# A fused attention and expert kernel: the last two units' means, values and products in another order, and a place of its own for unit 15's x

## The chip, the cores and the metric

The kernel runs on one core of a Trainium2 chip. The time is device time in microseconds (us) of one execution; the median of three is given. Engines are named as the profile names them: PE (TensorE, matmuls and transposes), DVE (VectorE), ACT (ScalarE), POOL (GpSimd) and SP (SyncE, which here only issues DMAs). SPq, ACTq and POOLq are the DMA issues of these engines.

## What is computed

Two stages, in float32:

```python
# attention: batch 8, heads 8, sequence 576, head size 64
q_d, k_d, v_d = means of q, k, v over 4 neighbours       # 144 rows
out = repeat(softmax(q_d k_d / 8) v_d, 4) + softmax(q k / 8, |i - j| < 4 only) v
x   = out.transpose(0, 2, 1, 3).reshape(4608, 512)
# experts: 4 groups of 4; every token goes to one
g   = argmax(x @ w_group);  e = argmax(x @ w_expert[g])
y   = softmax weights of both choices * (relu(x @ w1[g, e]) @ w2[g, e])
```

The result is y, 4608 x 512.

## The kernel before

**Attention by units.** The work of attention is cut into 16 units (2 batches and 2 heads each), numbered 0 to 15. A unit goes through named steps: scores (`s_local`, `s_down`), exponentials, and then, as far as it matters here:

- `down_store u` (L443) writes the unit's mean output `odn` to a table `odd` in DRAM: three DMAs on SP, two of 64 KB and one of 16 KB. `load_down u` (L450) reads it back in another layout, one DMA of 144 KB into eight-row strips of the tile `vw`.
- `load_windows u` (L211) loads the unit's values into the other rows of the same tile: two DMAs on SP of 378 KB each. Units 14 and 15 use the tiles vw0 and vw1.
- `turn_e u i` (L375) transposes a third of the local softmax weights `E` on PE, and `turn_e_out` copies it to `pt`. `x_bank u i` (L455) multiplies that third with `vw`: these are the value products, and since the means stand in `vw` as further rows, they add both parts of attention. `x_bank_out u i` (L464) copies the product to the tile `x`, `store_x` (L467) writes `x` to the DRAM table `xd`, and `turn_x`, `turn_x_out`, `logits` (L472 to L508) make the router's scores of it.

So `x_bank u` needs both `load_windows u` and `load_down u`, and `load_down u` can only be issued when `down_store u` has landed.

**The first expert, early.** When 12 units are in `xd`, 256 tokens of one small expert are fetched (`gather`, two indirect DMAs on POOL, L919) while attention still runs. `weights_in c` (L881) loads a quarter of the expert's two weights: two DMAs of 512 KB on SP, into two buffers that take turns. `weights_split c w` (L888) makes a high part on ACT (L891) and a low part on POOL or DVE (L892). `turn_in k` (L962) transposes a quarter of the tokens on PE, and ACT and DVE split it into `xh` and `xl` (L959, L960). `hidden f` (L971) is twelve matmuls on these; its third one, and every third, reads the low part of the weight. `project f` follows. Then the other 15 experts run in a loop that keeps PE busy to the end.

**What sets the order.** The string `ORDER` (L1387) names every step of attention, router and first expert in the order in which its instructions are recorded; each engine and each DMA queue then does its own instructions strictly in that order, with semaphores between the engines. A letter behind a step names the engine that copies (A, D, P) or the queue that issues (S is SP, A is ACT). Where a step waits, everything that is recorded behind it on the same engine waits too.

**Places.** `of(n, u)` (L114) picks the buffer of a unit: for units 14 and 15 it is always the first, so `x` of unit 15 goes where `x` of unit 14 stands, and may be written only when `store_x 14` has read it. `change` in `ORDER` gives the space of attention's inputs to the expert's weights.

Of the kernel before, what the change touches and what calls it, by code (L numbers as in the profile page):

```python
# [9 lines left out]
F32 = mybir.dt.float32  # L10
# [9 lines left out]
P = 128  # L20
B, H, S, D = 8, 8, 576, 64
SD = S // 4
G = 9
W = 38
WW = 42
# [11 lines left out]
NU = 4 * NB  # L37
# [23 lines left out]
class Attention:  # L61
# [9 lines left out]
    def __init__(self, tc, q, k, vm, vw, idf, xd, left, right, dram):  # L71
        nc = self.nc = tc.nc
        self.tc, self.q, self.k, self.vm_in, self.vw_in, self.idf = tc, q, k, vm, vw, idf
        cp = self.cp = left.enter_context(tc.tile_pool(name="attc", bufs=1))
        self.a1 = left.enter_context(tc.tile_pool(name="att1", bufs=1))
        self.a2 = left.enter_context(tc.tile_pool(name="att2", bufs=2))
        self.inp = right.enter_context(tc.tile_pool(name="inp", bufs=2, side="right"))
        self.odd = [dram.tile([2, 2 * SD, D], F32, name=f"odd{i}") for i in range(2)]
        self.st, self.banks, self.lg = {}, {}, {}
        self.turns = 0  # L80
        self.xd = xd
        self.kt = [self.inp.tile([P, 2, S], F32, name=f"kt{i}", bufs=1) for i in range(3)]
        self.kz = [self.inp.tile([P, 2, 2, S + 6], F32, name=f"kz{i}", bufs=1) for i in range(2)]
        self.load_k(0)
        self.load_q(0)
        self.mask = self.inp.tile([P, G, W], BF16, name="mask", bufs=1)
        self.vw = [(cp if i < 2 else self.inp).tile([P, 2, 2 * NBLK, D], F32, name=f"vw{i}", bufs=1) for i in range(3)]
        self.warm = self.inp.tile([P, 4 * P], BF16, name="warm", bufs=1)
        nc.vector.memset(self.warm, 0.0)
        one = cp.tile([1, 1], F32, name="one")  # L90
        nc.gpsimd.memset(one, 0.0)
        nc.scalar.activation(one, one, AF.Exp)
        self.zero = cp.tile([P, 1], F32, name="zero")
        nc.gpsimd.memset(self.zero, 0.0)
        self.idb = cp.tile([P, P], BF16, name="idb")
        self.vd = [self.inp.tile([P, 3, 2, D], F32, name=f"vd{i}", bufs=1) for i in range(2)]
        self.vs = [self.inp.tile([P, 3, 2, 4 * D], F32, name=f"vs{i}", bufs=1) for i in range(3)]
        self.mg = [cp.tile([P, 5], F32, name=f"mg{i}") for i in range(2)]
        self.sg = [cp.tile([P, 5, 2], F32, name=f"sg{i}") for i in range(2)]
        self.sd = [cp.tile([P, 5], F32, name=f"sd{i}") for i in range(2)]  # L100
        self.sl = [cp.tile([P, G, 2], F32, name=f"sl{i}") for i in range(2)]
        self.two = [cp.tile([P, G, 2, 2], F32, name=f"two{i}") for i in range(2)]
        self.rg = [cp.tile([P, 6], F32, name=f"rg{i}") for i in range(2)]
        self.kept = {}
        for n, more, shape in (
            ("pt", 1, [P, G * P]), ("x", 2, [P, G, P]), ("PdT", 1, [P, 3, 2 * SD]), ("od", 1, [P, 2 * SD]), ("odn", 1, [P, 3, 2, D])
        ):
            self.kept[n] = [cp.tile(shape, F32, name=f"{n}0")] + [self.inp.tile(shape, F32, name=f"{n}{i + 1}", bufs=1) for i in range(more)]
        self.E = [cp.tile([P, G, WW, 3], F32, name=f"E{i}") for i in range(2)]
        self.shares = self.inp.tile([P, 8], F32, name="shares", bufs=1)  # L110
        self.xT = cp.tile([P, 27 * P // 2], F32, name="xT")
        self.edge = self.inp.tile([P, 3, W], F32, name="edge", bufs=1)

    def of(self, n, u):  # L114

        t = self.kept[n]
        return t[u % len(t) if u < LATE_UNITS else 0]

# [1361 lines left out]
turn_pd_out 14 1 A; turn_x 12 2; store_x 12 A; turn_x_out 12 2 A; load_windows 14; soft_down 14; out_down 14; x_bank 13 1; s_down_max 15  # L1480
weight 2; s_down_exp 15 2; out_down_out 14 A; turn_down 14; x_bank 13 2; s_down_exp 15 0; s_down_exp 15 1; x_bank_out 13 1 A; pool_v 15
x_bank 13 0; turn_pd 15 0; x_bank_out 13 2 A; turn_down_out 14; soft_local 14; x_bank_out 13 0 A; turn_pd_out 15 0 A; places_out 2
store_x 13 A; turn_pd 15 1; down_store 14 S; turn_x 13 2; turn_pd 15 2; turn_pd_out 15 1 A; logits 12; turn_pd_out 15 2 D; load_windows 15
s_local_exp 15 1; turn_x_out 13 2 A; out_down 15; lists_places 2; turn_x 13 0; soft_down 15; turn_x 13 1; lists 2 P; out_down_out 15 A
turn_down 15; turn_x_out 13 1 A; turn_down_out 15; turn_x_out 13 0 A; load_down 14 S; down_store 15 S; early_expert; lists_add 2
turn_e 14 2; logits 13; turn_e 14 1; early_list 1; turn_e_out 14 2 A; change; gather; turn_e 14 0; lists_out 2; turn_e_out 14 1 A
turn_e_out 14 0 A; x_bank 14 2; x_bank 14 0; x_bank 14 1; x_bank_out 14 0 A; x_bank_out 14 1 A; turn_x 14 0; soft_local_sum 15
soft_local 15; x_bank_out 14 2 D; turn_e 15 0; store_x 14 A; turn_e_out 15 0 D; turn_x_out 14 0 D; turn_x 14 2; turn_x 14 1
turn_x_out 14 1 D; turn_x_out 14 2 A; weights_in 0; turn_e 15 1; turn_in 0; turn_e_out 15 1 D; weights_split 0 w1 P; load_down 15 S
logits 14; turn_in 1; weights_split 0 w2 P; weights_in 1; turn_e 15 2; turn_e_out 15 2 D; x_bank 15 0; turn_in 2; x_bank_out 15 0 A  # L1490
x_bank 15 1; x_bank_out 15 1 A; x_bank 15 2; x_bank_out 15 2 D; turn_in 3; weights_in 2; turn_x 15 1; turn_x 15 2; turn_x_out 15 2 D
store_x 15 S; turn_x 15 0; weights_split 1 w1 P; turn_x_out 15 1 D; turn_x_out 15 0 A; hidden 0; weights_split 1 w2 P; weights_in 3
logits 15; scores_out 3; hidden 1; scores_turn 3; project 0; scores_turn_out 3; choose 3; choose_exp 3; choose_first 3; weight 3; hidden 2
project 1; places 3; places_out 3; project 2; weights_split 2 w1 P; lists_places 3; lists 3 P; count 3; weights_split 2 w2 P; hidden 3
hidden 4; hidden 5; lists_add 3; early_list 0; gather_late; weights_split 3 w1 D; project 3; weights_split 3 w2 D; project 4; ranks
project 5; hidden 6; turn_late 0; turn_late 1; hidden 7; turn_late 2; turn_late 3; rank_lists; project 6; project 7
"""

@with_exitstack
# [111 lines left out]
```

## Time and profile before

| what | us |
|---|---|
| median of 3 runs | 681.47 |
| lowest and highest of them | 678.83, 684.85 |
| the profiled execution | 675.84 |
| its span, first to last instruction | 674.1 |

The profile is of one execution, with starts in us from the beginning of its span. The order of a row is start, duration, engine, line, operation, destination and source, shapes and count; rows of like instructions that follow each other are merged. A bracket at the end of a row says how long the engine was idle ahead of it and what ended that idle time. The steps of the change lie between about 201 and 224 us.

### The profile page before, as it was taken

The page shows a single profiled execution, that of the slowest core. Times are in us where ns is not written, and L with a number is a line of the kernel's source. Part 1 is how long each engine was busy: PE and PEld are TensorE (multiplying, and loading weights), DVE is VectorE, ACT ScalarE, POOL GpSimd, SP SyncE. Part 2 cuts the span into 40 slices and gives each one's busy share as a digit, 9 for nine tenths or more (in the row PEclk, how much of TensorE's full clock was granted, in tenths as well). Part 3 has the DMA queues.
Part 4 walks back from the last instruction along what each step waited for, and adds up shares of the span by engine and source line. Part 5 has one row for each costly group of instructions (what it writes and reads, how often), then busy time and mean ns, then how long its engine had stood idle before and what let it go on. Part 6 is the DMA issues. An engine that isn't in the chain of part 4 may idle for free. (4 is left out here: it accounts for less than half of the span.)

```text
span 674.1 us, 17810 instructions
## 1 busy us (share of the span) xinstructions
PE 641.1 (95%) x6750; PEld 576.3 (85%) x6751; DVE 478.3 (71%) x968; ACT 385.1 (57%) x831; POOL 362.9 (54%) x418
## 2 busy tenths in 40 slices
PE   7899998998986998999999999999999999999996
PEld 3676776776764886999999999999999999999985
DVE  5888788788896695556566676766777777787751
ACT  7887757666773535653545346464565556566531
POOL 8974754668621733404464746557456557555521
PEclk8999999998999998899999999999999999999999
DMA  8699899898878635768786969889889889999920
GB/s 321 199 288 298 250 306 292 234 256 263 231 198 274 180 98 194 238 216 194 228 254 191 256 213 260 224 270 268 255 264 276 255 278 300 252 295 289 280 71 29
DMA packets 125903, 160.75 MB, mean 238 GB/s; under 512 B 23133, under 2 KB 90601, under 8 KB 125792
## 3 DMA queue, kind: packets, MB, share of 16 engines
q1 hardware_dynamic: 100032, 130.01, 64.0%
q0 software_dynamic: 8240, 20.47, 10.3%
q10 hardware_dynamic: 17520, 8.85, 4.9%
q8 instruction: 62, 1.02, 0.7%
q14 instruction: 49, 0.40, 0.2%
HBM read 129.51 MB, written 30.98 MB: 238 GB/s over the span
## 5 line engine op out<-in xcount | busy, mean ns | idle before, releaser
L1057 POOL DMA_INDIRECT out_dram<-yt,qo x135 | 156.2, 1157 | 134.4 <-DVE qo L838 102.7
L985 ACT ACTIVATE hh<-ph 128x368 fp32r<-128x368 f32 (+14 forms) x128 | 53.0, 416 | 183.0 <-PE ph L981 179.2
L981 PE MATMUL ph<-xh,w1h 128*128 128x368 f32 (+14 forms) x512 | 152.6, 299 | 0.0
L981 PE MATMUL ph<-xl,w1h 128*128 128x368 f32 (+14 forms) x512 | 152.4, 298 | 0.0
L981 PE MATMUL ph<-xh,w1l 128*128 128x368 f32 (+14 forms) x512 | 152.3, 298 | 0.0
L1032 PE MATMUL y<-hh,w2h 128*128 128x368 f32 (+11 forms) x416 | 126.1, 303 | 0.0
L1032 PE MATMUL y<-hl,w2h 128*128 128x368 f32 (+11 forms) x416 | 125.7, 302 | 0.0
L1032 PE MATMUL y<-hh,w2l 128*128 128x368 f32 (+11 forms) x416 | 125.6, 302 | 0.0
L986 DVE SCALAR_TENSOR_TENSOR hl<-ph,hh 128x368 fp32r<-128x368 f32 (+14 forms) x128 | 58.7, 461 | 78.0 <-ACT hh L985 77.6
L981 PEld LDWEIGHTS ph<-xh,w1h 128*128 128x128 f32 x512 | 96.4, 189 | 1.0 <-issue 0.2
L981 PEld LDWEIGHTS ph<-xl,w1h 128*128 128x128 f32 x512 | 96.5, 188 | 0.8
L981 PEld LDWEIGHTS ph<-xh,w1l 128*128 128x128 f32 x512 | 96.5, 188 | 0.1
L892 DVE TENSOR_TENSOR w1l<-raww,w1h 128x1024 fp32r<-128x1024 f32 x61 | 74.6, 1224 | 25.2 <-ACT w1h L891 24.6
L892 DVE TENSOR_TENSOR w2l<-raww,w2h 128x1024 fp32r<-128x1024 f32 x61 | 74.7, 1224 | 23.9 <-ACT w2h L891 22.9
L919 POOL DMA_INDIRECT xg<-xd,gi x47 | 54.0, 1149 | 55.2 <-ACT xh L959 25.3
L1032 PEld LDWEIGHTS y<-hh,w2h 128*128 128x128 f32 x416 | 78.3, 188 | 0.0
L1032 PEld LDWEIGHTS y<-hh,w2l 128*128 128x128 f32 x416 | 78.3, 188 | 0.0
L1032 PEld LDWEIGHTS y<-hl,w2h 128*128 128x128 f32 x416 | 78.3, 188 | 0.0
L891 ACT ACTIVATE w1h<-raww 128x1024 fp32r<-128x1024 f32 x64 | 67.3, 1052 | 7.2 <-DMA raww<-in_moe_w_dram 3.4
L891 ACT ACTIVATE w2h<-raww 128x1024 fp32r<-128x1024 f32 x64 | 67.1, 1050 | 0.0
L960 DVE TENSOR_TENSOR xl<-xt,xh 128x256 fp32r<-128x256 f32 (+16 forms) x68 | 30.4, 449 | 15.5 <-ACT xh L959 15.4
L460 PE MATMUL b_x<-vw,pt 126*32 126x128 f32 x1152 | 37.8, 275 | 2.1 <-DMA vw<-odd 1.6
(243 smaller groups left out, 1189.1 us busy)
## 6 DMA issues: line engine op xcount, KB each, us to landing
raww<-in_w2q_dram SPq DMA_DIRECT2D x52, 512.0 KB
raww<-in_w1q_dram SPq DMA_DIRECT2D x52, 512.0 KB
raww<-in_moe_w_dram SPq DMA_DIRECT2D x24, 512.0 KB
vw<-in_vw_dram SPq DMA_DIRECT2D x32, 378.0 KB
kt<-in_k_dram SPq DMA_DIRECT2D x16, 576.0 KB
qT<-in_q_dram SPq DMA_DIRECT2D x16, 576.0 KB
xd<-x ACTq DMA_DIRECT2D x15, 576.0 KB
vs<-in_vm_dram SPq DMA_DIRECT2D x16, 512.0 KB
```

The lines of the kernel that those rows point to most:

```text
L460: self.nc.tensor.matmul(pt[32 * j : 32 * j + 32, t], self.of("pt", u)[:ROWS, 32 * lin : 32 * lin + 32], self.windows(u)[:ROWS, :, lin], st ...
L891: self.nc.scalar.activation(hi, raw, AF.Copy)
L892: eng.tensor_tensor(out=lo, in0=raw, in1=hi.bitcast(F32), op=ALU.subtract)
L919: self.nc.gpsimd.indirect_dma_start(out=xg[:w], out_offset=None, in_=self.xd[0:rows], in_offset=bass.IndirectOffsetOnAxis(ap=st["gi"][:w, ...
L960: self.nc.vector.tensor_tensor(out=lo, in0=x, in1=hi.bitcast(F32), op=ALU.subtract)
L981: nc.tensor.matmul(ph, a[:, k, cs], st[b][:, k, 0:C], start=(n == 0), stop=(n == 11))
L985: nc.scalar.activation(hh, ph, AF.Relu)
L986: nc.vector.scalar_tensor_tensor(out=hl, in0=ph, scalar=0.0, in1=hh.bitcast(F32), op0=ALU.max, op1=ALU.subtract)
L1032: nc.tensor.matmul(y, a[:, f % 2, cs], b, start=(f == 0 and n == 0), stop=(f == 7 and n == 2))
L1057: i = self.nc.gpsimd.indirect_dma_start(out=out, out_offset=bass.IndirectOffsetOnAxis(ap=index, axis=0), in_=y, in_offset=None, bounds_che ...
```

## The change

Three things change, in the order string and in one buffer.

1. `load_windows 15` moves behind `load_down 14`, and `load_down 15` moves ahead of `weights_in 0` and `weights_in 1` (it stood between them). These are issues on SP's queue.
2. `x` of unit 15 goes into the space of `E0`, which unit 14 used and which is free once unit 14's `E` is transposed. `E0` grows from 1134 to 1152 floats per partition for that.
3. The value products, their copies and the transposes of units 14 and 15 stand in another order; all of `x_bank 15` stands ahead of `turn_in 0`, and `store_x 15` ahead of `weights_in 2`.

```diff
-        self.E = [cp.tile([P, G, WW, 3], F32, name=f"E{i}") for i in range(2)]
+        flat = [cp.tile([P, G * (P if i == 0 else 3 * WW)], F32, name=f"E{i}") for i in range(2)]
+        self.E = [x[:, 0 : G * 3 * WW].rearrange("p (g w e) -> p g w e", g=G, e=3) for x in flat]
+        self.last_x = flat[0].rearrange("p (g f) -> p g f", g=G)
...
     def of(self, n, u):
 
+        if n == "x" and u == NU - 1:
+            return self.last_x
...
-turn_x_out 14 1 D; turn_x_out 14 2 A; weights_in 0; turn_e 15 1; turn_in 0; turn_e_out 15 1 D; weights_split 0 w1 P; load_down 15 S
...
+turn_e 15 1; turn_e_out 15 1 A; turn_e 15 2; turn_e_out 15 2 A; turn_x_out 14 0 D; load_down 15 S; weights_in 0; weights_in 1; x_bank 15 0
+x_bank_out 15 0 A; x_bank 15 1; x_bank_out 15 1 D; logits 14; x_bank 15 2; x_bank_out 15 2 A; store_x 15 S; turn_in 0; weights_split 0 w1 P
...
```

The lines of the changed kernel are numbered four higher than those of the kernel before, from L120 on.

**SP's queue, before**, from the windows of unit 15 (vw1) to the first quarter of the weights (raww10 and raww20); odd0 and odd1 are the DRAM tables of the means of units 14 and 15:

```order
L214 DMA vw1_104<-in_vw_dram 42x2x1152 x2
L453 DMA vw0_103<-odd0_92 8x4x1152
L447 DMA odd1_93<-odn0_140 128x2x64 x2
L448 DMA odd1_93<-odn0_140 32x2x64
L1535 TENSOR_LOAD eri0_183
L1535 ISA x2
L886 ISA
L886 DMA raww10_3839<-in_moe_w1_dram 128x4x256
L886 ISA
L886 DMA raww20_3840<-in_moe_w2_dram 128x2x512
L453 DMA vw1_104<-odd1_93 8x4x1152
```

and in the changed kernel:

```order
L457 DMA vw0_103<-odd0_92 8x4x1152
L218 DMA vw1_104<-in_vw_dram 42x2x1152 x2
L451 DMA odd1_93<-odn0_140 128x2x64 x2
L452 DMA odd1_93<-odn0_140 32x2x64
L1539 TENSOR_LOAD eri0_183
L1539 ISA x2
L457 DMA vw1_104<-odd1_93 8x4x1152
L890 ISA
L890 DMA raww10_3839<-in_moe_w1_dram 128x4x256
```

Unit 14's means (vw0<-odd0) now stand ahead of unit 15's windows, unit 15's means (vw1<-odd1) ahead of all weights, and the store of unit 15's means (odd1<-odn0) behind both transfers it stood beside.

**PE, before**, from the first transposes of the gathered tokens (xt<-xg) to the last of unit 15's x (b_xt); b_e is `turn_e`, b_x is `x_bank`, with the third and the unit as its numbers:

```order
L966 MATMUL xt_3954<-idf_60,xg_3867 128x128 x2
L505 MATMUL lg_147<-xT_145,wr_151 32x256 x4
L966 MATMUL xt_3967<-idf_60,xg_3867 128x128 x2
L379 MATMUL b_e_2_15_3976<-idf_60,E1_143 126x128 x3
L460 MATMUL b_x_0_15_3981<-vw1_104,pt0_131 32x128 x12
L966 MATMUL xt_3994<-idf_60,xg_3867 128x128 x2
L460 MATMUL b_x_1_15_4000<-vw1_104,pt0_131 32x128 x12
L460 MATMUL b_x_2_15_4014<-vw1_104,pt0_131 32x128 x12
L966 MATMUL xt_4028<-idf_60,xg_3867 128x128 x2
L475 MATMUL b_xt_1_15_4036<-idf_60,x0_133 128x128 x3
L475 MATMUL b_xt_2_15_4040<-idf_60,x0_133 128x128 x3
L475 MATMUL b_xt_0_15_4046<-idf_60,x0_133 128x128 x3
```

and in the changed kernel:

```order
L383 MATMUL b_e_2_15_3952<-idf_60,E1_143 126x128 x3
L464 MATMUL b_x_0_15_3963<-vw1_104,pt0_131 32x128 x12
L464 MATMUL b_x_1_15_3977<-vw1_104,pt0_131 32x128 x12
L509 MATMUL lg_147<-xT_145,wr_151 32x256 x4
L464 MATMUL b_x_2_15_3995<-vw1_104,pt0_131 32x128 x12
L970 MATMUL xt_4010<-idf_60,xg_3867 128x128 x2
L479 MATMUL b_xt_0_15_4017<-idf_60,E0_142 128x128 x3
L479 MATMUL b_xt_1_15_4022<-idf_60,E0_142 128x128 x3
L970 MATMUL xt_4027<-idf_60,xg_3867 128x128 x2
L479 MATMUL b_xt_2_15_4034<-idf_60,E0_142 128x128 x3
L970 MATMUL xt_4039<-idf_60,xg_3867 128x128 x2
L970 MATMUL xt_4046<-idf_60,xg_3867 128x128 x2
```

All transposes of the gathered tokens now stand behind all three value products of unit 15; unit 15's x is read from E0.

**ACT, before**, from the copies of unit 14's x to the split of the second quarter of the tokens:

```order
L178 ACTIVATE x0_133<-b_x_0_14_3894 128x384
L178 ACTIVATE x0_133<-b_x_1_14_3907 128x384
L470 DMA xd_65<-x0_133 128x9x128
L178 ACTIVATE xT_145<-b_xt_2_14_3938 128x3x128
L959 ACTIVATE xh_3865<-xt_3954 128x256
L891 ACTIVATE w1h0_3843<-raww10_3839 128x1024
L959 ACTIVATE xh_3865<-xt_3967 128x256
L891 ACTIVATE w2h0_3845<-raww20_3840 128x1024
```

and in the changed kernel, from the copy of the last third of unit 14's x:

```order
L182 ACTIVATE x0_133<-b_x_0_14_3913 128x384
L474 DMA xd_65<-x0_133 128x9x128
L182 ACTIVATE xT_145<-b_xt_2_14_3909 128x3x128
L182 ACTIVATE pt0_131<-b_e_1_15_3947 126x384
L182 ACTIVATE pt0_131<-b_e_2_15_3952 126x384
L182 ACTIVATE E0_142<-b_x_0_15_3963 128x384
L182 ACTIVATE E0_142<-b_x_2_15_3995 128x384
L963 ACTIVATE xh_3865<-xt_4010 128x256
L895 ACTIVATE w1h0_3843<-raww10_3839 128x1024
```

The high part of the first weight (w1h0) now stands behind two copies of unit 15's x, which in turn wait for that unit's value products.

## Rows read from the trace of the kernel before

**Rows 1.** The page: its span, and a row of the DMA issues (count, size each).
```profile
span 674.1 us, 17810 instructions
...
raww<-in_moe_w_dram SPq DMA_DIRECT2D x24, 512.0 KB
```

**Rows 2.** Windows, 210 to 220 us: length, busy PE, PEld, DVE, ACT, POOL; PEclk, DMA, GB/s.
```profile
210.00:215.00 5.00, 3.47 (x68) 2.86 (x58) 2.16 (x5) 1.48 (x3) 0.84 (x1) 1.00 1.00 333
215.00:220.00 5.00, 3.19 (x60) 2.12 (x64) 1.78 (x4) 2.77 (x5) 1.36 (x1) 1.00 1.03 334
```

**Rows 3.** Timeline of PE, 206 to 224 us.
```profile
206.72 0.87 PE L379 MATMUL b_e<-idf,E 128*126 128x128 f32 x6
209.20 2.17 PE L460 MATMUL b_x<-vw,pt 126*32 126x128 f32 x72 [1.61 <-DMA vw<-odd]
...
212.68 0.49 PE L379 MATMUL b_e<-idf,E 128*126 128x128 f32 x3
214.63 0.30 PE L966 MATMUL xt<-idf,xg 128*128 128x128 f32 x1 [1.46 <-DVE xT L180]
216.81 0.33 PE L966 MATMUL xt<-idf,xg 128*128 128x128 f32 x1 [1.88 <-DMA xg<-xd,gi]
217.07 0.64 PE L505 MATMUL lg<-xT,wr 128*32 128x256 f32 x8
217.64 0.44 PE L966 MATMUL xt<-idf,xg 128*128 128x128 f32 x2
...
218.34 0.86 PE L460 MATMUL b_x<-vw,pt 126*32 126x128 f32 x24
...
221.98 1.20 PE L475 MATMUL b_xt<-idf,x 128*128 128x128 f32 x9 [0.59 <-ACT x L178]
...
223.25 0.28 PE L981 MATMUL ph<-xh,w1l 128*128 128x256 f32 x1
```

**Rows 4.** Timeline of SP's DMA issues, 201 to 210 us.
```profile
201.45 1.20 SPq L448 DMA_DIRECT2D odd<-odn  x1
202.75 1.71 SPq L214 DMA_DIRECT2D vw<-in_vw_dram  x2
205.24 0.68 SPq L453 DMA_DIRECT2D vw<-odd  x1
206.01 0.90 SPq L447 DMA_DIRECT2D odd<-odn  x2
206.97 0.46 SPq L448 DMA_DIRECT2D odd<-odn  x1
208.64 0.98 SPq L886 DMA_DIRECT2D raww<-in_moe_w_dram  x2
209.73 0.77 SPq L453 DMA_DIRECT2D vw<-odd  x1
```

**Rows 5.** What SP waited for, 200 to 212 us: total, times, longest.
```profile
SPq L453 <- DMA odd<-odn: 0.6, 1, 0.6
```

**Rows 6.** Timeline of ACT, 217 to 222 us.
```profile
217.23 0.38 ACT L959 ACTIVATE xh<-xt 128x256 fp32r<-128x256 f32 x1 [4.18 <-PE xt L966]
217.51 1.05 ACT L891 ACTIVATE w1h<-raww 128x1024 fp32r<-128x1024 f32 x1
...
221.05 0.87 ACT L178 ACTIVATE x<-b_x 128x384 f32<-128x384 f32 x2 [1.00 <-DMA xd<-x]
```

**Rows 7.** Timeline of POOL: first low part of a weight, and the fifth.
```profile
218.64 2.39 POOL L892 TENSOR_TENSOR w1l<-raww,w1h 128x1024 fp32r<-128x1024 f32 x1 [7.80 <-ACT w1h L891]
...
231.69 2.40 POOL L892 TENSOR_TENSOR w1l<-raww,w1h 128x1024 fp32r<-128x1024 f32 x1 [3.27 <-ACT w1h L891]
```

**Rows 8.** Windows around 263 us, columns as in rows 2.
```profile
259.60:263.00 3.40, 1.08 (x4) 0.41 (x3) 2.33 (x3) 3.40 (x6) 0.28 (x1) 1.00 0.69 228
263.00:266.40 3.40, 3.24 (x11) 2.49 (x12) 1.56 (x3) 2.09 (x5) 0.00 (x0) 0.50 0.58 186
...
273.20:276.60 3.40, 3.40 (x20) 3.40 (x20) 0.67 (x3) 1.50 (x4) 2.45 (x3) 1.00 0.60 201
```

More of the change, by code (lines that the diff above doesn't have):

```diff
@@ L1482 @@
 x_bank 13 0; turn_pd 15 0; x_bank_out 13 2 A; turn_down_out 14; soft_local 14; x_bank_out 13 0 A; turn_pd_out 15 0 A; places_out 2
-store_x 13 A; turn_pd 15 1; down_store 14 S; turn_x 13 2; turn_pd 15 2; turn_pd_out 15 1 A; logits 12; turn_pd_out 15 2 D; load_windows 15
-s_local_exp 15 1; turn_x_out 13 2 A; out_down 15; lists_places 2; turn_x 13 0; soft_down 15; turn_x 13 1; lists 2 P; out_down_out 15 A
-turn_down 15; turn_x_out 13 1 A; turn_down_out 15; turn_x_out 13 0 A; load_down 14 S; down_store 15 S; early_expert; lists_add 2
+store_x 13 A; turn_pd 15 1; down_store 14 S; turn_x 13 2; turn_pd 15 2; turn_pd_out 15 1 A; logits 12; turn_pd_out 15 2 D; s_local_exp 15 1
@@ L1486 @@
+turn_x_out 13 2 A; out_down 15; lists_places 2; turn_x 13 0; soft_down 15; turn_x 13 1; lists 2 P; out_down_out 15 A; turn_down 15
+turn_x_out 13 1 A; turn_down_out 15; turn_x_out 13 0 A; load_down 14 S; load_windows 15; down_store 15 S; early_expert; lists_add 2
 turn_e 14 2; logits 13; turn_e 14 1; early_list 1; turn_e_out 14 2 A; change; gather; turn_e 14 0; lists_out 2; turn_e_out 14 1 A
-turn_e_out 14 0 A; x_bank 14 2; x_bank 14 0; x_bank 14 1; x_bank_out 14 0 A; x_bank_out 14 1 A; turn_x 14 0; soft_local_sum 15
@@ L1488 @@
-soft_local 15; x_bank_out 14 2 D; turn_e 15 0; store_x 14 A; turn_e_out 15 0 D; turn_x_out 14 0 D; turn_x 14 2; turn_x 14 1
-turn_x_out 14 1 D; turn_x_out 14 2 A; weights_in 0; turn_e 15 1; turn_in 0; turn_e_out 15 1 D; weights_split 0 w1 P; load_down 15 S
-logits 14; turn_in 1; weights_split 0 w2 P; weights_in 1; turn_e 15 2; turn_e_out 15 2 D; x_bank 15 0; turn_in 2; x_bank_out 15 0 A
-x_bank 15 1; x_bank_out 15 1 A; x_bank 15 2; x_bank_out 15 2 D; turn_in 3; weights_in 2; turn_x 15 1; turn_x 15 2; turn_x_out 15 2 D
@@ L1492 @@
[L1492 to L1495, printed above, removed]
@@ L1496 @@
-project 5; hidden 6; turn_late 0; turn_late 1; hidden 7; turn_late 2; turn_late 3; rank_lists; project 6; project 7
+turn_e_out 14 0 A; x_bank 14 2; x_bank_out 14 2 A; x_bank 14 1; x_bank_out 14 1 A; turn_x 14 2; x_bank 14 0; x_bank_out 14 0 A; turn_x 14 1
+store_x 14 A; soft_local_sum 15; soft_local 15; turn_x_out 14 2 A; turn_x 14 0; turn_e 15 0; turn_e_out 15 0 D; turn_x_out 14 1 D
+turn_e 15 1; turn_e_out 15 1 A; turn_e 15 2; turn_e_out 15 2 A; turn_x_out 14 0 D; load_down 15 S; weights_in 0; weights_in 1; x_bank 15 0
@@ new lines @@
+x_bank_out 15 0 A; x_bank 15 1; x_bank_out 15 1 D; logits 14; x_bank 15 2; x_bank_out 15 2 A; store_x 15 S; turn_in 0; weights_split 0 w1 P
+turn_x 15 0; turn_x_out 15 0 D; turn_x 15 1; turn_x_out 15 1 A; turn_in 1; weights_split 0 w2 P; turn_x 15 2; turn_x_out 15 2 D; turn_in 2
+weights_in 2; turn_in 3; weights_split 1 w1 P; hidden 0; weights_split 1 w2 P; weights_in 3; logits 15; scores_out 3; hidden 1
+scores_turn 3; project 0; scores_turn_out 3; choose 3; choose_exp 3; choose_first 3; weight 3; hidden 2; project 1; places 3; places_out 3
@@ L1497 @@
+project 2; weights_split 2 w1 P; lists_places 3; lists 3 P; count 3; weights_split 2 w2 P; hidden 3; hidden 4; hidden 5; lists_add 3
+early_list 0; gather_late; weights_split 3 w1 D; project 3; weights_split 3 w2 D; project 4; ranks; project 5; hidden 6; turn_late 0
+turn_late 1; hidden 7; turn_late 2; turn_late 3; rank_lists; project 6; project 7
 """
```

## The prediction

> **What bounds the kernel now.** I read the span first: 674.1 us of the profiled execution's 675.84 [rows 1]. The busy shares of the page help little here, because the change touches some 20 us; what counts is which wait of PE ends last there. So the second view is the timeline of PE [rows 3]. The reader is to see three holes in it: 1.61 us ahead of unit 14's value products at 209.20, which end when the means of unit 14 land; 1.46 and 1.88 us around the first transposes of the gathered tokens at 214.63 and 216.81 (the second hole ends when the gather lands); and 0.59 us ahead of unit 15's transposes at 221.98, where PE waits for ACT. From 217.07 PE has work for the rest of the stage, and the first expert's hidden products read the low part of a weight for the first time at 223.25. I call that instant M; from there on PE is busy almost without a break, so what M gains or loses is what the kernel gains or loses. The holes hold 5.5 us in all, and that is the most the change could give.
>
> The third view is SP's queue [rows 4]. It shows issues, their length, and by the next issue when a wait ended. Unit 14's means are issued at 205.24, after a wait of 0.6 us for the landing of their own store [rows 5], whose last piece went out at 201.45: 3.79 us from issue to landing. Unit 15's means go out at 209.73, 2.76 us after the last piece of their store (206.97). The fourth view is the windows: from 210 to 220 us the DMA engines are full at 333 and 334 GB/s [rows 2].
>
> **The change, part by part.** Nothing is computed less: the same matmuls, copies and DMAs, in another order. Each part is worth what it does to M.
>
> *Unit 14's means ahead of unit 15's windows.* Their issue waits for the landing of the store, which the windows do not hold up much, so I leave it at 205.24. What goes is 756 KB in front of them. From issue to the first product it took 3.96 us before (205.24 to 209.20 [rows 3, 4]). PE has unit 14's transposes done at 207.59 (206.72 + 0.87), so at most 1.61 us are to be had here, at least none. I book it at nothing: what PE gains, it loses ahead of unit 15's products, next.
>
> *Unit 15's means ahead of the weights.* This sets the new M. On SP: unit 14's means end at 205.92 (205.24 + 0.68); the two windows take 1.71, to 207.7; the three stores take 1.42 as before (206.01 to 207.43), the last of them issued at 208.7. Their landing is what SP waits for next. At 2.76 us it comes at 211.5, at 3.79 us at 212.5. I take 211.5, since the pair of rows for this very store gives it; the queue ahead of it is the same windows, only closer. Then the means: 3.96 us to the first product, as for unit 14, which was the one read with PE waiting for it. So x_bank 15 starts at T = 211.5 + 3.96 = 215.4. Lower end: 2.76, the shortest wait between an issue and a landing among the rows, T = 214.2. Upper end: before, the product at 218.34 found the means landed [rows 3], 8.6 us after the issue at 209.73, with two weights of 512 KB [rows 1] ahead in SP's queue; at 333 GB/s those are 3.1 us, so 5.5 us at most without them; on the later 212.5 this gives T = 218.0. Until T PE has only unit 14's rest: its products (2.12 us), transposes of x, and unit 15's transposes, which ended at 213.17 (212.68 + 0.49) with one of three still to do. PE then waits about 2 us, so the hole stays.
>
> *All value products ahead of the first turns.* From T: 2.12 us for the 72 products, 0.57 for the logits among them (217.07 to 217.64), so turn_in 0 at T + 2.7. Before, from that transpose to the end of the low part on POOL it took 4.2 us: 216.81, ACT's copy at 217.23, high part at 217.51, low part 218.64 to 221.03 [rows 3, 6, 7]. Now ACT has the last copy of unit 15's x (about 0.45 us) in front, which ends 0.3 us later than xh would have begun. So the low part is there at T + 7.2, and M = T + 7.25 = 222.7. Before, M was 223.25: **0.5 us gained**. The break-even is T = 216.0. Note what changed hands: before, the low part was ready 2.2 us before M, and PE was late; now PE reaches the hidden products at about T + 5.3 and waits for POOL.
>
> *Unit 15's x in its own place.* Before, ACT waited 1.00 us at 221.05 for the store of unit 14's x, and PE 0.59 us behind it [rows 3, 6]. Both waits go. Inside the new M they are worth nothing of their own, as ACT's copies now stand ahead of turn_in 0; without the new place, those copies would wait for that store, and M with them.
>
> *Weights later.* weights_in 0 is issued after unit 15's means, at about 212.3 where it was 208.64. ACT asks for the first at T + 3.6 = 219.0. Even if all of it comes last (gather 540 KB, means 144 KB, unit 14's x 576 KB, the weight 512 KB: 1.8 MB), at 333 GB/s it is through at 217. Cover: 2 us; gone, M would follow the weight one for one. Behind it, the third quarter waits for POOL to free its buffer, 1.6 us later than before; POOL's fifth low part, at 231.69, waited 3.27 us for ACT in its turn and not for a DMA [rows 7], which covers the 1.6. Costed at nothing. store_x 15 goes out earlier and is waited for by the late gather only, well behind M: nothing.
>
> **Sum**: 0.5 us off the profiled execution, 675.3. The median of the three runs, 681.47, is 5.6 us above that execution; I take the same 0.5 off it: **681.0 us**. A measurement of this kernel can tell about 1% (6.8 us) from no change.
>
> **A rule against the trace.** The rows above give 3.96 us for reading the means and 2.76 to 3.79 for storing them. The Trainium skill, page "DMA: Bandwidth & Descriptors", section "Anatomy of one DMA — SWDGE (gpsimd) path", puts a DMA at some 2.0 us plus its bytes by 436 GB/s, most of the 2 us being the receipt of the last write, and says that a wait on a semaphore is made by the issuing sequencer. By it, as an estimate, SP would stand still for 2.0 us for the store and the means would take 2.3, and T would be 213.1; the trace has both longer, so the sum goes by the trace.
>
> **The rivals.**
>
> *Slower: the means of unit 15 come late.* Unit 14's x is now stored, and the tokens gathered, just while the means are in flight; the DMA engines were full there before [rows 2]. From T = 216.0 the change costs time, one for one, with SP, ACT and POOL queued behind: at T = 218.0 M is 225.25, 2.0 us later: 683.5. For it: store and means are two DMAs in a row that nothing else can hide now. Against it: the weights, 2 MB, are out of the way. If the first weight is the late one, the time is about the same. 0.2.
>
> *Faster: nothing is late.* If stores and means land at their shortest, PE never waits at unit 15's products: T is about 213.2, when PE is done with unit 14, M = 220.45, a gain of 2.8: 678.7. For it: no transfer stands ahead of the means in SP's queue. Against it: no row shows them under 3.96 us. The Trainium skill's page named above would have it so. 0.15.
>
> *The clock moves.* At 263 us, after a stretch in which PE was busy 1.08 of 3.4 us, the granted clock fell from 2.4 to 1.2 GHz, and three windows ran at half (the first of the three stands in the rows): 11 matmuls in 3.4 us where 20 ran at full clock [rows 8], so about 4.6 us in all. Between 213.17 and 216.81 PE had 0.3 us of work, and the clock held [rows 2, 3]. The new order has two holes of about 2 us (ahead of T, and ahead of M) instead. A fall there costs up to 4.6 us: 685.6; one avoided in runs where it falls now gives 4.6: 676.4. The Trainium skill, "TensorE: Matmul & The Clock Gate", section "HAM oscillation — how this bites in real kernels", warns of matmul bursts between DMA waits, which fall back to half clock; of the two stretches here the trace agrees for one. 0.05 each way.
>
> **How the numbers follow.** The forecast, M moved by -1.75 to +1 us, has 0.55; slower 0.2, faster 0.15, the clock 0.1. The bounds of T alone give 679.7 to 683.5. With the clock's 4.6 us either way, and the three runs shown lying 3 us to each side of their median, I take 676 to 685.5. None of the cases reaches 1%; only the clock together with such scatter does: faster by over 1% 0.05, slower 0.03, within 1% 0.92.
>
> **What would show it.** In the profile after: unit 14's means issued at about 205.2, ahead of the windows; unit 15's means at 211 to 212.5, ahead of the weights; the hole of PE ahead of turn_in 0 gone and one ahead of x_bank 15, ended by the means; turn_in 0 some 2.7 us after that; the first low part on POOL ready at about 222.6, and PE waiting for it with the third hidden product; no wait of ACT for the store of x. A shift at M that is not found again some 20 us later would prove the path wrong. So would a first product of unit 15 that waits for something other than its means, or a hidden product that waits for a weight.

## The result, and the profile after

| | before | changed |
|---|---|---|
| median, us | 681.65 (677.07 to 686.05, 16 runs) | 686.80 (682.81 to 691.27, 16 runs) |
| ratio, 95% interval | 1 | 1.0085 (1.0063 to 1.0108) |

By the medians the change costs 5.2 us. The forecast was 681.0 and no change, with a range up to 685.5: it was wrong, in size and in sign. Two later sets of six runs of the changed kernel, on two chips, gave 1.0103 and 1.0133.

The page after, span:

```profile
span 681.1 us, 17811 instructions
```

SP's issues in the changed kernel (timeline), to be read against [rows 4]:

```profile
203.28 0.71 SPq L457 DMA_DIRECT2D vw<-odd  x1
204.09 1.69 SPq L218 DMA_DIRECT2D vw<-in_vw_dram  x2
...
206.92 0.45 SPq L452 DMA_DIRECT2D odd<-odn  x1
211.05 0.75 SPq L457 DMA_DIRECT2D vw<-odd  x1
212.14 2.62 SPq L890 DMA_DIRECT2D raww<-in_moe_w_dram  x4
```

The order is the one predicted. Unit 15's means (211.05) wait 4.13 us for the landing of their store (206.92); 2.76 was forecast. All starts are some 2 us early here: unit 14's first transpose of `E` stands at 203.78, and stood at 205.72. In the 17 profiles of this document it lies between 203.78 and 208.77, and two runs of one kernel (`e9_after_split_early`, `e14_early_again`) differ by 1.9 us, so I take the difference for scatter. From here on I call that transpose A and count from it.

PE in the changed kernel (timeline), against [rows 3]:

```profile
203.78 0.49 PE L383 MATMUL b_e<-idf,E 128*126 128x128 f32 x3
...
215.92 2.26 PE L464 MATMUL b_x<-vw,pt 126*32 126x128 f32 x48 [3.68 <-issue]
217.89 1.15 PE L509 MATMUL lg<-xT,wr 128*32 128x256 f32 x8
218.74 1.46 PE L464 MATMUL b_x<-vw,pt 126*32 126x128 f32 x24
220.13 0.44 PE L970 MATMUL xt<-idf,xg 128*128 128x128 f32 x2
...
223.38 0.28 PE L985 MATMUL ph<-xl,w1h 128*128 128x256 f32 x1
224.48 0.39 PE L985 MATMUL ph<-xh,w1l 128*128 128x256 f32 x1 [0.82 <-POOL w1l L896]
...
233.77 0.48 PE L1034 MATMUL y<-w2h,hh 128*128 128x512 f32 x1
237.35 0.80 PE L1034 MATMUL y<-w2h,hl 128*128 128x512 f32 x1 [3.11 <-DVE hl L990]
```

T, the first product of unit 15, is A + 12.14 (forecast: 215.4 against A at 205.72, so A + 9.68). M, the first read of a low part, is A + 20.70 (before A + 17.53), and it waits for POOL, as forecast. The bracket at T names no releaser (`issue` is time in which the engine waited for nothing that the profile shows). But the last copy of `pt` that these products read ended at 212.77 (ACT), and the trace's last record of the landing of unit 15's means is at 215.83, 0.09 us ahead of T; so T waited for the means. Then the row that no step had: at 237.35 PE has stood 3.11 us for DVE, in the middle of the third project. Two windows of the changed kernel (columns as in [rows 2]) show the granted clock at its lower level, 1.2 GHz, behind the first hole and partly behind the second:

```profile
216.50:219.90 3.40, 3.40 (x68) 3.04 (x59) 0.56 (x1) 0.49 (x1) 0.00 (x0) 0.50 1.07 365
236.00:241.00 5.00, 3.65 (x14) 3.17 (x15) 4.75 (x16) 0.00 (x0) 2.06 (x1) 0.66 0.14 18
```

ACT in the changed kernel (timeline), against [rows 6]: the copies of unit 15's x no longer wait for the store, and the first high part stands behind them.

```profile
216.95 0.49 ACT L182 ACTIVATE E<-b_x 128x384 f32<-128x384 f32 x1 [4.18 <-PE b_x L464]
220.26 0.49 ACT L182 ACTIVATE E<-b_x 128x384 f32<-128x384 f32 x1 [2.81 <-PE b_x L464]
220.65 0.38 ACT L963 ACTIVATE xh<-xt 128x256 fp32r<-128x256 f32 x1
220.93 1.05 ACT L895 ACTIVATE w1h<-raww 128x1024 fp32r<-128x1024 f32 x1
```

POOL in the changed kernel (timeline), against [rows 7]: first, fourth and fifth low part, and the first gather for the loop.

```profile
222.07 2.36 POOL L896 TENSOR_TENSOR w1l<-raww,w1h 128x1024 fp32r<-128x1024 f32 x1 [13.19 <-ACT w1h L895]
...
229.08 2.41 POOL L896 TENSOR_TENSOR w2l<-raww,w2h 128x1024 fp32r<-128x1024 f32 x1
233.63 2.36 POOL L896 TENSOR_TENSOR w1l<-raww,w1h 128x1024 fp32r<-128x1024 f32 x1 [2.14 <-ACT w1h L895]
...
258.03 1.03 POOL L923 DMA_INDIRECT xg<-xd,gi  x1 [9.55 <-DVE none L802]
```

DVE in the changed kernel (timeline). From `mx` to `cw` it is the router of the last tokens: the largest score, then comparisons and sums of at most 180 numbers a partition. `ge` and `sel` are steps on the way to its list of rows `gi`.

```profile
228.78 0.42 DVE L990 SCALAR_TENSOR_TENSOR hl<-ph,hh 128x256 fp32r<-128x256 f32 x1 [1.97 <-ACT hh L989]
229.14 0.34 DVE L603 TENSOR_REDUCE mx<-lg 128x45 f32<-128x180 f32 x1
229.51 2.18 DVE L604 TENSOR_TENSOR t<-lg,mx 128x180 f32<-128x180 f32 x1
231.61 0.33 DVE L605 TENSOR_TENSOR ex<-lg,mx 128x180 f32<-128x180 f32 x1
...
233.59 0.20 DVE L673 TENSOR_TENSOR tw<-sums,o 128x36 f32<-128x36 f32 x1
233.70 2.32 DVE L674 TENSOR_SCALAR two<-sums 128x9 f32<-128x9 f32 x1
...
236.88 0.42 DVE L990 SCALAR_TENSOR_TENSOR hl<-ph,hh 128x256 fp32r<-128x256 f32 x1
...
237.88 0.21 DVE L645 TENSOR_TENSOR ge<-pos,steps 128x45 f32<-128x45 f32 x1
...
245.70 0.27 DVE L792 TENSOR_TENSOR sel<-tv,early 128x64 f32<-128x64 f32 x1
...
246.26 0.17 DVE L796 TENSOR_SCALAR gi<-rv 128x4 int32<-128x4 f32 x1
```

and the same steps in the kernel before:

```profile
227.80 0.34 DVE L599 TENSOR_REDUCE mx<-lg 128x45 f32<-128x180 f32 x1
228.18 0.45 DVE L600 TENSOR_TENSOR t<-lg,mx 128x180 f32<-128x180 f32 x1
...
230.64 0.16 DVE L670 TENSOR_SCALAR two<-sums 128x9 f32<-128x9 f32 x1
...
231.72 0.42 DVE L986 SCALAR_TENSOR_TENSOR hl<-ph,hh 128x256 fp32r<-128x256 f32 x1
...
233.14 1.01 DVE L641 TENSOR_TENSOR ge<-pos,steps 128x45 f32<-128x45 f32 x1
...
239.44 0.84 DVE L788 TENSOR_TENSOR sel<-tv,early 128x64 f32<-128x64 f32 x1
...
240.57 0.17 DVE L792 TENSOR_SCALAR gi<-rv 128x4 int32<-128x4 f32 x1
```

Two short instructions stand 2.18 and 2.32 us where they took 0.45 and 0.16, and neither shows a wait ahead of it. Look at when they end: 231.69 and 236.02. POOL's fourth low part ends at 231.49 (229.08 + 2.41), its fifth at 235.99. DVE stands inside the instruction until POOL has finished its own. `hl`, which the third project needs, is behind both in DVE's queue, and so is the router's list of rows `gi`, which the late gather waits for. I call this the collision. In the kernel before, the fourth low part was the one at 226.03 and ended at 228.42, just as `t` began; the fifth began at 231.69 [rows 7], when `two` was done:

```profile
226.03 2.39 POOL L892 TENSOR_TENSOR w2l<-raww,w2h 128x1024 fp32r<-128x1024 f32 x1 [0.32 <-ACT w2h L891]
...
237.28 2.92 POOL L892 TENSOR_TENSOR w2l<-raww,w2h 128x1024 fp32r<-128x1024 f32 x1
...
252.32 1.04 POOL L919 DMA_INDIRECT xg<-xd,gi  x1 [9.54 <-PE phr L997]
```

The kernel before has collisions of its own, on other rows. `ge` stands 1.01 us there and ends at 234.15, the fifth low part at 234.09; `sel` stands 0.84 us and ends at 240.28, the sixth low part at 240.20. In the changed kernel the two take 0.21 and 0.27. So the change moves the collision: DVE stands 3.89 us longer in `t` and `two` and 1.37 us less in `ge` and `sel`.

The last row of the POOL timeline of before (252.32) is the first of the four gathers of the loop's first expert, G: A + 46.60 before. In the changed kernel it stands at 258.03, A + 54.25. Of the 7.65 us between, 3.17 lie ahead of M, 0.11 from M to the router's first row (4.55 and 4.66 us), 4.35 from there to `gi` (12.77 and 17.12 us) and 0.02 behind it. Of the 4.35, 2.52 are the instructions just named; the rest comes back to DVE from PE, whose later products are late by its hole: between the three `hl` ahead of `gi` DVE waits twice 0.99 us, where they followed each other without a wait before. The spans of the two executions differ by 7.0 us: A is 1.94 us earlier in the changed one, and 1.29 us come behind G.

### The profile page after: what moved, and what is told of

The parts are those of the page before. It is cut to its first block, busy times and chain, and to the rows that moved or that the text cites. A ratio compares the mean times of both kernels' runs of the same rounds, so it can differ in the third digit from the quotient of the medians.

```text
span 681.1 us, 17811 instructions
## 1 busy us (share of the span) xinstructions
PE 642.4 (94%) x6751; PEld 576.6 (85%) x6751; DVE 477.7 (70%) x965; ACT 384.8 (56%) x834; POOL 364.5 (54%) x418
## 5 line engine op out<-in xcount | busy, mean ns | idle before, releaser
L923 POOL DMA_INDIRECT xg<-xd,gi x47 | 55.6, 1183 | 55.6 <-ACT xh L963 24.0
L464 PE MATMUL b_x<-vw,pt 126*32 126x128 f32 x1152 | 39.6, 281 | 5.9 <-issue 4.1
L464 PEld LDWEIGHTS b_x<-vw,pt 126*32 126x32 f32 x1152 | 31.5, 112 | 11.7 <-issue 8.2
```

Of the source, the lines that this page charges most:

```text
L464: self.nc.tensor.matmul(pt[32 * j : 32 * j + 32, t], self.of("pt", u)[:ROWS, 32 * lin : 32 * lin + 32], self.windows(u)[:ROWS, :, lin], st ...
L923: self.nc.gpsimd.indirect_dma_start(out=xg[:w], out_offset=None, in_=self.xd[0:rows], in_offset=bass.IndirectOffsetOnAxis(ap=st["gi"][:w, ...
```

## The experiments

Two theories. **Lock**: the loss is the collision; POOL's low parts come later against the router, DVE stands for them, and PE and the list stand behind DVE. **Means**: the loss lies ahead of M, in the late means of unit 15 and the half clock behind them. Later a third, **order**: the new order costs something in another stretch. The expectations call `t` the router's subtraction (it is the comparison with the largest score), and `two` the small add.

All edits are in the order string unless they say otherwise. Each group ran on one chip beside its own runs of the kernel before; their medians were 684.27, 675.16, 681.33 and 677.00 us.

**First group: one part each.**

`e1_split_dve`: the changed kernel, the fourth and fifth low part on DVE.

```diff
-weights_split 1 w2 P; weights_in 3; ... project 2; weights_split 2 w1 P
+weights_split 1 w2 D; weights_in 3; ... project 2; weights_split 2 w1 D
```

> The changed kernel, but the low parts of the second w2 quarter and of the third w1 quarter are made on DVE instead of POOL. Lock theory (the loss comes mainly where POOL's low parts, now 1 to 3 us later, meet the router's small DVE instructions: two of them stood 2.2 and 2.3 us instead of 0.4 and 0.2, each to the end of a POOL instruction, and PE then waited 3.1 us for the second hidden product's low part): these two DVE rows fall back to 0.4 and 0.2 us, PE's hole of 3.1 us and the half clock behind it go, and the kernel is 3 to 5 us faster than the changed one, within 0.3% of the kernel before. Means theory (the loss comes ahead of the first hidden product, because unit 15's means land late and the clock falls in that hole): the time stays at that of the changed kernel, 1.008 times the kernel before, or a little above, as DVE has 2.4 us more to do.

1.0047 (1.0017 to 1.0078). `t` took 0.35 and `two` 0.17 us; but the low part that DVE took over stood 2.89 us itself, beside POOL's third, and came ahead of the router, and PE waited 2.19 us for the lists later on. The collision was moved rather than taken away.

`e2_pool_late`: the kernel before, POOL's first low part computed twice.

```diff
         eng.tensor_tensor(out=lo, in0=raw, in1=hi.bitcast(F32), op=ALU.subtract)
+        if (c, n) == (0, "w1") and "r" not in st:
+            eng.tensor_tensor(out=lo, in0=raw, in1=hi.bitcast(F32), op=ALU.subtract)
```

> The kernel before, with POOL's very first low part made twice over, so that all of POOL's later ones come 2.4 us later; loads, ACT and PE keep their order, and the first use of a low part had 2.2 us of slack. Lock theory: the first use moves by less than 0.5 us, but POOL's fourth low part now lies over the router's first DVE instructions, one of which stands 1 to 2 us; the kernel is 1.5 to 4 us slower than before (1.002 to 1.006). Means theory: nothing, within 0.5 us of the kernel before.

1.0020 (0.9982 to 1.0058). Both long rows appear in the old order, 1.55 and 2.34 us, and PE's hole of 2.67 with them. The interval cannot tell that from nothing; see the last group but one.

`e3_old_loads`: the changed kernel with SP's order of before.

```diff
-load_down 14 S; load_windows 15; down_store 15 S; ... load_down 15 S; weights_in 0; weights_in 1
+load_windows 15; ... load_down 14 S; down_store 15 S; ... weights_in 0; load_down 15 S; weights_in 1
```

> The changed kernel with SP's order of the kernel before: unit 15's windows early, its means between the first two weights; the new place of x and the new order on PE, ACT and DVE stay. Means theory: the order of the loads is the cause, so the time comes back to the kernel before (1.000 to 1.002). Lock theory: ACT's high part still stands behind unit 15's value products, which wait for means that land at about 216 us, so POOL's low parts stay late and the kernel stays slower than before by 3 us or more (1.005 and up).

1.0028 (0.9993 to 1.0062). M is at A + 17.09, ahead of the 17.53 of before, so nothing is lost ahead of it; the long rows (2.17 and 2.33) and the hole (3.11) stand all the same. The new loads are not what makes the collision.

`e4_new_loads`: the kernel before with the new order of loads (the reverse of that edit).

> The kernel before with SP's order of the changed kernel alone: unit 14's means ahead of unit 15's windows, unit 15's means ahead of all weights. Means theory: slower than before by 2 to 5 us (1.003 to 1.008), since the means and the weights behind them come late. Lock theory: the first high part still hangs on the gather alone, so POOL is on time and the kernel is within 1 us of the kernel before.

0.9991 (0.9960 to 1.0021). The means are not late here: the first product of unit 15 stands at A + 10.16 and waits 0.18 us. What is late is the first weight. ACT waits 4.16 us for it, PE 3.46 us behind that ahead of the third product, and M is at A + 19.54:

```profile
219.03 1.06 ACT L891 ACTIVATE w1h<-raww 128x1024 fp32r<-128x1024 f32 x1 [4.16 <-DMA raww<-in_moe_w_dram]
```

The rows on DVE are short (0.45 and 0.17): the fourth low part waits for ACT and ends at 230.40, as `t` begins at 230.15. The new loads alone cost at most 1.4 us.

**Second group: second profiles, and an edit that failed.**

> The kernel before, unchanged, for a second profile of it. Lock theory (the loss comes from the low parts on POOL meeting the last router's instructions on DVE): in the old order POOL is ahead of TensorE, so the first subtraction of the last router stands 0.35 to 0.5 us and its first small add 0.17 us, and from the last router's first subtraction to the end of its list of rows 12.4 us pass, as in the first profile (228.18 to 240.74). If both stand over 2 us here too, the lock is in the kernel before as well and is not what the change adds. Means theory (the loss lies ahead of the first hidden product): says nothing of these rows; the first product that reads a low part stands 17 to 18 us after unit 14's first transpose of means (17.5 in the first profile).

Short rows again (0.45, 0.17), M at A + 18.90, list 12.77 us behind the router's first row: the collision with `t` and `two` is not in the kernel before. The one with `ge` and `sel` is, with 1.01 and 0.84 us as in its first profile.

> The changed kernel, unchanged, for a second profile and beside the two that follow. Both theories: 1.006 to 1.011 of before. Both long rows on DVE, 2.0 to 2.4 us each, and the hole of some 3 us ahead of the third project's second product stand again; the value products of unit 15 start some 12 us after unit 14's first transpose of means.

1.0103 (1.0057 to 1.0150), rows of 2.18 and 2.33 us, hole 3.11, T at A + 12.62.

`e7_after_low0_dve` and `e8_old_loads_low0_dve`: the first low part on DVE, in the changed kernel and in `e3_old_loads`.

```diff
-turn_in 0; weights_split 0 w1 P
+turn_in 0; weights_split 0 w1 D
```

> The changed kernel with the first of the eight low parts of the weights on DVE (1.2 us there, DVE is idle at that point) instead of POOL (2.4 us). Lock theory: POOL is through with its remaining three about 2.4 us earlier, so the last router's subtraction stands under 0.8 us instead of 2.2, its small add 0.2 instead of 2.3, the hole ahead of the third project goes, the first product of a low part comes 1.1 us earlier: 5.5 us less than the changed kernel, 0.999 to 1.002 of before. Means theory: the first low part is read 1.1 us earlier and that is all: 1.005 to 1.008.

> The same edit on the changed kernel with the load order of before (own place for x and the new order of TensorE's and ScalarE's work only). Lock theory: no long rows on DVE, the first product of a low part some 16 us after unit 14's first transpose of means (17.5 before, 17.1 with the old loads and POOL), 3 us less than that kernel's 1.0028: 0.996 to 0.999, ahead of both kernels. Means theory: that kernel's 1.0028 less the 1.1 us: 1.000 to 1.002.

1.0115 (1.0064 to 1.0166) and 1.0101 (1.0065 to 1.0136). The edit did not do what both theories had it do. DVE's low part stood in front of a copy of unit 15's transposed x, PE waited 0.91 us for that copy, and POOL still began only when ACT gave it the second high part. DVE and POOL of `e8_old_loads_low0_dve` (timelines):

```profile
228.19 1.62 DVE L604 TENSOR_TENSOR t<-lg,mx 128x180 f32<-128x180 f32 x1
...
231.82 2.33 DVE L674 TENSOR_SCALAR two<-sums 128x9 f32<-128x9 f32 x1
```

```profile
227.21 2.40 POOL L896 TENSOR_TENSOR w2l<-raww,w2h 128x1024 fp32r<-128x1024 f32 x1
231.75 2.38 POOL L896 TENSOR_TENSOR w1l<-raww,w1h 128x1024 fp32r<-128x1024 f32 x1 [2.14 <-ACT w1h L895]
```

As a test of the collision's removal it says nothing. What `e8_old_loads_low0_dve` does show: old loads, M at A + 17.16, ahead of before's 17.53 and 18.90, and 1.0% slower. The means theory has nothing to explain that with.

**Third group: POOL early, by ACT's order alone.** `e9_after_split_early` moves the first four splits up in the changed kernel; ACT makes the first two high parts between its copies of unit 15's x. The orders of PE, DVE, POOL and SP stay. `e10_old_loads_split_early` does the like in `e3_old_loads`, with the first one ahead of both copies.

```diff
-x_bank_out 15 0 A; x_bank 15 1; x_bank_out 15 1 D; logits 14; ... turn_in 0; weights_split 0 w1 P
+x_bank_out 15 0 A; weights_split 0 w1 P; x_bank 15 1; x_bank_out 15 1 D; weights_split 0 w2 P; logits 14; ... turn_in 0; weights_split 1 w1 P
-turn_in 1; weights_split 0 w2 P; ... turn_in 3; weights_split 1 w1 P; hidden 0; weights_split 1 w2 P
+turn_in 1; ... turn_in 3; weights_split 1 w2 P; hidden 0
```

> The changed kernel with the splits of the first two eighths' weights moved up on ScalarE and POOL alone (the orders of TensorE, DVE and SP stay): the first pair stands between the copies of unit 15's x instead of behind them, the second pair ahead of the first hidden product. Lock theory: POOL starts its low parts 3 us or more earlier and has ended the first four when the last router begins, so its subtraction stands under 0.5 us, its small add 0.2, the hole ahead of the third project goes, and from the router's first row to the list of rows 12.8 us pass instead of 16.8 to 18.4; 4.5 to 5.5 us less than the changed kernel: 1.000 to 1.003 of before. Means theory: only the 0.8 us wait of the first hidden product for POOL goes: 1.007 to 1.009.

> The same move with the load order of before, so that unit 15's means are not late either: the new place for x, the new order of TensorE's work, and the splits early. Lock theory: no long rows on DVE, first product of a low part 16 us after unit 14's first transpose of means (17.5 and 18.9 in the two profiles of before): 0.994 to 0.999, ahead of both kernels. Means theory: 1.000 to 1.002, as for the old loads without this move (1.0028, and 1.0101 with one part on DVE) less 1 us. If the long rows go and the time stays at 1.01, both fall.

> The kernel before with one low part of the weights computed twice on POOL (the earlier run of it: 1.0020, with both long rows on DVE, 1.55 and 2.34 us, and 17.9 us from router to list instead of 12.8). Run again beside the others because the chips differ. Lock theory: POOL 2.4 us late is enough: 1.005 to 1.009 here, with no other change at all. Means theory: 1.000 to 1.003.

1.0074 (1.0039 to 1.0110), 1.0033 (0.9993 to 1.0073) and 1.0093 (1.0052 to 1.0135). In the first two the long rows and the hole are gone (`t` 0.35, `two` 0.17 us), and G is at A + 48.58 and A + 45.76, yet their times went down less than that. By time alone `e9_after_split_early` fits the means theory and `e10_old_loads_split_early` lies above both ranges; no run of the changed kernel stands beside them in this group. In `e9_after_split_early` the edit also brought a wait of its own: ACT stood 1.49 us for the first weight, in front of a copy of unit 15's x, and PE 1.87 us behind that copy. The third has nothing but a POOL that is 2.4 us late in the old order, and is 0.9% slower, with the long rows of the changed kernel to a hundredth. Its DVE (timeline):

```profile
227.79 2.18 DVE L600 TENSOR_TENSOR t<-lg,mx 128x180 f32<-128x180 f32 x1
...
231.97 2.33 DVE L670 TENSOR_SCALAR two<-sums 128x9 f32<-128x9 f32 x1
```

**Fourth group: the four kernels side by side**, since chips differ.

> The kernel before, unchanged, once more: a null comparison (0.997 to 1.003) and a third profile, on the same chip as the three that follow, so that their stretches can be set against it. Both theories: clean rows on DVE (0.45 and 0.17 us), some 47 us from unit 14's first transpose of means to the first of the four gathers.

> The kernel with the old loads and the early splits again (first run 1.0033, interval 0.9993 to 1.0073, long rows gone, gather 0.8 us earlier after unit 14's first transpose than in the first profile of before). Lock theory: the collision was the loss, so without it 0.997 to 1.001. Order theory, new: the new order of TensorE's work costs 1.5 to 2.5 us of its own somewhere else, which would show as a longer stretch behind the gather or ahead of unit 14's transpose: 1.002 to 1.005.

> The changed kernel with the early splits again (first run 1.0074, interval 1.0039 to 1.0110, long rows gone, gather 2.0 us later than in the first profile of before). Lock theory with the late means beside it: 1.002 to 1.004, at least 4 us under the changed kernel. Order theory: 1.005 to 1.008, and 1 to 2 us under the changed kernel.

> The changed kernel, unchanged, beside the two without long rows: 1.007 to 1.011, with the two rows of 2.2 and 2.3 us and the gather 52 to 56 us after unit 14's first transpose. Lock theory: 4 us or more over the changed kernel with early splits; order theory: 1 to 2 us over it.

From the traces: M, from the router's first row (`mx`) to `gi`, and G, all in us; G and M from A.

| kernel | ratio (interval) | M | mx to gi | G | t, two |
|---|---|---|---|---|---|
| before, `e12_before_third` | 0.9990 (0.9959 to 1.0021) | 18.10 | 12.77 | 47.21 | 0.45, 0.17 |
| early splits, old loads, `e13_early_old_again` | 0.9990 (0.9954 to 1.0026) | 17.26 | 12.77 | 46.39 | 0.34, 0.17 |
| changed, early splits, `e14_early_again` | 1.0021 (0.9987 to 1.0054) | 21.26 | 12.76 | 50.37 | 0.35, 0.17 |
| changed, `e15_after_third` | 1.0133 (1.0091 to 1.0176) | 21.53 | 17.30 | 55.24 | 2.19, 2.32 |

The last two differ in ACT's order and in when POOL begins, and in nothing else. Their POOL (timelines, first the early one):

```profile
224.70 2.36 POOL L896 TENSOR_TENSOR w1l<-raww,w1h 128x1024 fp32r<-128x1024 f32 x1 [11.21 <-ACT w1h L895]
...
231.70 2.40 POOL L896 TENSOR_TENSOR w2l<-raww,w2h 128x1024 fp32r<-128x1024 f32 x1
238.09 2.40 POOL L896 TENSOR_TENSOR w1l<-raww,w1h 128x1024 fp32r<-128x1024 f32 x1 [3.99 <-ACT w1h L895]
```

```profile
223.24 2.36 POOL L896 TENSOR_TENSOR w1l<-raww,w1h 128x1024 fp32r<-128x1024 f32 x1 [14.03 <-ACT w1h L895]
...
230.27 2.41 POOL L896 TENSOR_TENSOR w2l<-raww,w2h 128x1024 fp32r<-128x1024 f32 x1
234.81 2.37 POOL L896 TENSOR_TENSOR w1l<-raww,w1h 128x1024 fp32r<-128x1024 f32 x1 [2.14 <-ACT w1h L895]
```

The early one's A is at 208.39 and M at 229.65; its fourth low part ends at 234.10, and `t` begins at 234.57. The other's M is 225.65, its fourth ends at 232.68, and `t` began at 230.69. Between the two, G differs by 4.87 us and the time by 1.0133 - 1.0021 = 0.0112 of 677 us, 7.6 us (3.9 to 11.3, the intervals taken together). The two profiled executions themselves are only 1.85 us apart (679.45 and 681.30), as A comes 4.27 us later in the early one; the price in time rests on the 12 and 6 runs. What `e14_early_again` has left above before is 0.2%, with an interval that holds zero (0.7% in `e9_after_split_early`). It may come from M, A + 21.26 against 17.26 with the old loads; that is not shown.

So the lock theory stands. On one chip and side by side, the collision with `t` and `two` went when POOL began earlier, and 1.1% with it; and a late POOL alone, in the old order, brought the collision and 0.9%. The late means are a smaller part, which no run tells from nothing: `e14_early_again` is 0.3% above `e13_early_old_again` (-0.2 to 0.8%, the intervals taken together). The order theory has little left: with old loads and early splits the new order is about as fast as before (0.9990 and 1.0033), though some tenths of a per cent are not excluded. No version beat both kernels. Two things stay open. The collision's price in time is not pinned down: 4.9 us in the trace, 3.9 to 11.3 in this group, less in the first group (1.0020 and 1.0028 with the long rows, where the same kernel or the nearest to it gave 1.0093 and 1.0101 elsewhere); no profile of the kernel before exists from that first chip. And of the late means, that the store takes 4.13 us to land rather than 2.76 was not taken apart further. In the seven other profiles with the new loads SP waits 3.19 us (`e4_new_loads`, the old order of PE) and 4.11 to 5.02 us (the new order of PE) for this landing.

## Why the prediction was wrong

- **The step that failed is "Weights later ... Costed at nothing"**, and with it the sentence that what M gains or loses is what the kernel gains or loses. I followed POOL's low parts to the fifth's wait for ACT and asked whether they are late for PE. I did not ask what else runs while they do. The arithmetic was in the trace: when PE waits for POOL, M is the end of the first low part, the fourth ends three times 2.35 us later, at M + 7.0, and the router's first comparison comes at M + 4.9 (before, `t` at 228.18 and M at 223.25). I had even written that POOL was 2.2 us ahead at M and would be so no longer, and costed that at nothing. It cost 4.35 us from the router to its list, and M to G grew by 4.48. The prediction had named the sign: a shift at M that is not found again later. M moved by 3.17 us and G by 7.65.
- **T was mis-sized**: A + 12.14 instead of 9.68. Of the 2.46 us, 1.37 are the landing of the store (4.13 for 2.76, above even the 3.79 at the upper end), 0.91 the means themselves (211.05 to 215.92 is 4.87, for 3.96), the rest the issues that stand ahead of them on SP. T was at the upper end of the bounds here, and 0.3 and 0.9 us past it in `e6_after_again` and `e14_early_again`. The rival "the means of unit 15 come late" happened, and M, forecast 0.5 us earlier, came 3.17 us later than in the first profile of before (1.8 and 2.6 later than in the other two). Its price, 2.0 us, is neither confirmed nor refuted: 0.3% (-0.2 to 0.8%) between `e13_early_old_again` and `e14_early_again`.
- **The range took one rival at a time.** Late means and the clock both came, in the same execution; by the prediction's own prices that is 683.5 + 4.6 = 688.1, past the range's end. A range with both would have held 686.80 by luck only, since neither rival is the collision.
- **A small DMA's time.** The rows of before had 2.76 us for the store and 3.96 for the means, and 4.13 and 4.87 came. The Trainium skill's page "DMA: Bandwidth & Descriptors", section "Anatomy of one DMA — SWDGE (gpsimd) path", with its 2.0 us plus bytes by 436 GB/s, was further off than the rows; that section is about DMAs that GpSimd issues, and these are SP's.
- **The clock**: it fell behind the hole ahead of T, as that rival had it. M - T is 8.56, forecast 7.25, and 6.88 in `e3_old_loads`, whose granted clock stays at 1.00 there; so up to M the half clock cost some 1.3 to 1.7 us (an estimate from these rows) and not up to 4.6. It fell a second time behind the hole of the third project. Both falls follow waits; `e14_early_again` has the first fall too and is 0.2% slower only.
- **Own place for x, products ahead**: as forecast. ACT's wait and PE's 0.59 us behind it are gone, M waits for POOL; alone, with the old loads (`e3_old_loads`), they bring M to A + 17.09, from 17.53, 18.10 and 18.90 in the three profiles of before, and no time.
- **What a page said against it.** The rows first: `t` and `two` stand until POOL ends, while `mx`, a reduction, and `hl`, which reads its `ph` from PSUM (where matmuls put their results), take their usual 0.34 and 0.42 us beside POOL at 229.14 and 228.78. It goes the other way round too: POOL's sixth low part, begun in the kernel before at 237.28 while DVE's `m` ran to 237.93, took 2.92 us instead of 2.36 to 2.41. The Trainium skill, page "SBUF — State Buffer", section "Who interferes with whom", says that VectorE and GpSimd share a pair of ports, held for a whole instruction; a VectorE instruction with two SBUF inputs meets a GpSimd instruction that reads SBUF, a `tensor_scalar` may, a `tensor_reduce` never does: "Issue order, not op shape, decides who blocks." The traces agree with each of these; the prediction did not draw on them.

## What to carry to other kernels

When a change makes an off-path engine late, do not stop at "is its result late for the one who waits for it". Lay its whole run of instructions over what the other engines do in that time; where one engine stands inside an instruction until another has ended its own, as DVE did beside POOL here, no semaphore shows the wait, only a duration. An instruction that takes many times its usual time and ends just as the other engine's does is the sign to look for.

An experiment that is meant to take a cause away must be read for whether it did: the first low part on DVE left the collision in place, and its time alone would have spoken against the right theory.

## What the hardware showed

- A DVE instruction on 9 elements a partition stood 2.32 us, some 14 times its 0.16, beside one POOL instruction of 2.36 us; the same in the other kernels with the collision (2.32 to 2.34).
- It goes for DVE's long instructions too: a low part that takes 1.22 us alone took 2.89 beside one on POOL in `e1_split_dve`.
- Small DVE instructions collide in the kernel before as well: 45 and 64 elements a partition stood 1.01 and 0.84 us (`ge`, `sel`) instead of 0.21 and 0.27, each until a POOL instruction ended.
- A store of 64, 64 and 16 KB had landed 4.13 us after its last issue, with 288 GB/s moving meanwhile (206.9 to 211.1 us); before, it had landed within 2.76, with 141 GB/s moving. The traffic alone does not explain it: in `e4_new_loads` it had landed within 3.19, with 316 GB/s.
